# Local attention with a gated MoE layer: the attention's four PSUM banks as two tiles of two, its copies by tile, and the stages in a new order

## The chip, the cores and the metric

The kernel runs on one core of a Trainium2 chip. The metric is the device time of one execution in microseconds (us). The engines are TensorE (PE, matrix products), VectorE (DVE), ScalarE (ACT), GpSimd (POOL) and SyncE (SP, which issues the DMAs here). SBUF is the on-chip memory, PSUM the eight banks of 2 KB per partition into which TensorE writes.

## The reference, cut to what matters

For 8 batches of 8 heads, 512 local and 32 global positions and head size 64, attention with a window of 32 and global keys, then a gated layer on the joined heads:

```python
s_g  = scale * q_g @ k_all.T                    # 32 global queries see all 544 keys
out_g = softmax(s_g) @ v_all
s_ll = where(abs(i - j) <= 32, scale * q_l @ k_l.T, -1e9)
s_l  = concat([scale * q_l @ k_g.T, s_ll])      # local queries see a band and the 32 global keys
out_l = softmax(s_l) @ concat([v_g, v_l])
x = concat([out_g, out_l]) as [8, 544, 512]
h = relu(x @ w_in)                              # 512 -> 1024
conv = a depthwise filter of three taps along the sequence over h
out = (h * sigmoid(conv)) @ w_out               # 1024 -> 512
```

Here `x` is [8, 544, 512] because the 32 global rows and the 512 local rows of the 8 heads of 64 are joined.

## The kernel before, in words

The work is cut into small stages, each a function that issues some instructions; `n` counts heads (0 to 63, eight to a batch), `u` units of the gated layer, `o` its outputs. The attention of two heads at a time: LQ and LV load, **S** computes the scores (32 x 2 small matmuls into two banks, one for each head), **M** masks them on DVE out of PSUM (four operations with their row minimum, tile `negm`), **E** is the exp on ACT, **NS** and **NP** normalize (NP on POOL in the first batch, on ACT later), **DT** transposes blocks on DVE, **P** multiplies with the values (112 matmuls into four banks). The result of P is split into two fp32r parts: **XH** copies it on ACT into `xh`, **XL** subtracts on DVE into `xl`. For the global queries, once a batch: **G** (scores, four banks), **GM**, **GE**, **GN** (softmax), **GT** (transposes, two banks), **GC** (copy), **GP** (times values), **GO** (tile `og`), **GQ** (moves rows, into the bank beside GP's) and **GX** (splits them into `xh` and `xl`).

The gated layer: per batch and half of the sequence, eight units **PZ** (12 matmuls of 128 x 274 each, the product with `w_in` in three fp32r parts), **RE** (relu, ACT), **C1** (POOL), **Ca** and **Cb** (DVE; the three taps), **TH** (tanh, ACT, over two units), **GG** (DVE), **GH** (ACT) and **GL** (DVE or POOL; the split of `g`); then four outputs of two halves **Oa** and **Ob** (12 matmuls each), **OE** (copy, DVE) and **ST** (store). In the first 110 us, eight blocks of weights (`w_in`, then `w_out`) are loaded (WD) and split: WA, WH and WX on ACT, **WC** and **WL** on DVE, **WS** on PE.

All attention stages write one PSUM tile `four` of four banks (line 73), of which a planner hands out two halves of two banks. S, GT and GP take a half, G and P take both. The other four banks belong to a pool `ps` for PZ, O and WS. The tile framework derives the waits between instructions from the tiles they use.

The order of all stages on all engines is made ahead by a planner in the kernel (`plan`, `arranged`): each stage has an engine, a cost, predecessors, slots that it takes and frees, and a place from the tables `POS` (batches from the second on) and `POS0` (first batch and weights). `arranged` walks through time and starts on each engine the ready stage with the least place. `emit` issues the stages in that order and chains each engine's instructions in it; every engine, and SP's queue of DMAs, then runs strictly in order.

Of the kernel before, what the change touches and what calls it, by code (L numbers as in the profile page):

```python
# [11 lines left out]
F32 = mybir.dt.float32  # L12
# [6 lines left out]
P = 128  # L19
H = 8  # L20
# [31 lines left out]
def f(ap):  # L52
    return ap.bitcast(F32)
# [3 lines left out]
def attn_moe(ctx: ExitStack, tc: tile.TileContext, qk_d, vw_d, qg_d, w_in_d, w_out_d, cw_d, out_d):  # L57
# [221 lines left out]
    def SC(n):  # L279

        qk = heads[n]["qk"]
        k = SIDE["S", n] * 2
        for j in range(2):
            heads.setdefault(n + j, {})["s"] = four[:, k + j, :].rearrange("p (r x) -> p r x", r=NR)
        for r in range(NR):
            for c in range(4):
                i = NR * c + r
                a = SL + (NK * c + r) * SG
                for j in range(2):
                    rows = slice(j * D, (j + 1) * D)  # L290
                    nc.tensor.matmul(  # L291
                        heads[n + j]["s"][c * SG : (c + 1) * SG, r, :], lhsT=qk[rows, i * SG : (i + 1) * SG],
                        rhs=qk[rows, a : a + P], start=True, stop=True,
                    )

    def G(n):

        first = n - 7
        g = [groups.setdefault(2 * (n // H) + j, {}) for j in range(2)]
        for j in range(2):  # L300
            g[j]["s0"], g[j]["s1"] = four[:, j, :], four[:, 2 + j, 0:SG]
        for i in range(3):
# [68 lines left out]
    def XH(n):  # L371
        b, h = divmod(n, H)
        xh, xl = x_of(b, h // 2)
# [31 lines left out]

    def GT(n):
        gr = groups[n // 4]
        k = 2 * SIDE["GT", n]
        gr["t"] = four[:, k : k + 2, :].rearrange("p a x -> p (a x)")[:, 0 : NG * P]
# [9 lines left out]
    gos = {}  # L419

    def GP(n):
        b, k = n // H, 2 * SIDE["GP", n]
        po, pt = gos[b] = [four[:, k, 0 : 2 * D].rearrange("p (a d) -> p a d", a=2), four[:, k + 1, 0 : 4 * SG]]
# [123 lines left out]
    def ST(o):  # L547
# [2 lines left out]
        nc.sync.dma_start(out=out_d[b, mt, :, half * HALF : (half + 1) * HALF], in_=outs[o])  # L550

    emit(tc, B, dict(
        LQ=LQ, LV=LV, LG=LG, G=G, S=SC, M=MA, E=EX, NS=NS, NP=NP, DT=DT, P=PV, XH=XH, XL=XL,
        GM=GM, GE=GE, GN=GN, GT=GT, GC=GC, GP=GP, GO=GO, GQ=GQ, GX=GX,
        PZ=Z, RE=RE, C1=C1, Ca=lambda u: C2(u, 0), Cb=lambda u: C2(u, 2), TH=TH, GG=GG, GH=GH, GL=GL,
        Oa=lambda o: O(o, 0), Ob=lambda o: O(o, 1), OE=OE, ST=ST, WD=WD, WA=WA, WC=WC, WH=WH, WL=WL, WS=WS, WX=WX,
# [8 lines left out]
LIMIT = dict(h=2, o=2)  # L565

ENG = dict(
    XH="a", GC="a", GX="v", NP="a", RE="a", C1="p", GH="a", GL="v", OE="v", WA="a", WH="a", WX="a",
)
ENG0 = dict(  # L570
    XH="a", GC="a", GX="v", NP="p", RE="a", C1="p", GH="a", GL="p", OE="v", WA="a", WH="a", WX="a",
)

POS = dict(
    LQ=0.17, LG=-1.2, LV=8.05, S=-2.21, M=-18.29, E=219.57, NS=25.61, NP=295.34, DT=213.15, P=-133.05, XH=1.69,
    XL=-26.65, G=20.61, GM=45.55, GE=48.47, GN=-59.02, GP=-13.22, GX=48.92, PZ=21.78, RE=58.89, C1=-4.96,
    Ca=71.38, Cb=-23.21, TH=33.51, GG=-1.1, GH=-42.18, GL=39.36, Oa=143.85, Ob=115.21, OE=-11.46, ST=-82.81,
    WD=52.48, WA=25.01, WC=1.49, WH=74.51, WL=1.52, WS=45.66, WX=6.65, GC=38.39, GO=-50.79, GQ=16.06, GT=25.45,
)
# [14 lines left out]
def cost(key, e):  # L594
# [40 lines left out]
    if key == "NP":  # L635
# [29 lines left out]
def plan(B):  # L667
# [31 lines left out]
    for n in range(N):  # L699
# [26 lines left out]
        if h == H - 1:  # L726
            ks = [f"qk{p - 3 + c}" for c in range(4)]
            ga = ["ga%d" % b, "gb%d" % b]
# [22 lines left out]
def units(op, late, b):  # L751
    for half in range(2):
# [3 lines left out]
        for ft in range(NFT):  # L756
# [5 lines left out]
            ready = [("XL", 8 * b + h) for h in range(0, H, 2)]  # L762
# [13 lines left out]
        for mt in range(NCT):  # L776
# [7 lines left out]
            at_o("Ob", [("Oa", o), ("GL", 8 * hh + 5), ("GL", 8 * hh + 7)], [], [f"o{o}"] + g)  # L784
            at_o("OE", [("Ob", o)], [("o", f"ot{o}")], [f"o{o}", f"o{o}o"])
            at_o("ST", [("OE", o)], [], [f"ot{o}"])


def arranged(ops, sides=None):
# [26 lines left out]
    while events:  # L816
# [9 lines left out]
        for e in (PE, DVE, ACT, POOL, SP):  # L826
# [123 lines left out]
```

## Time and profile before

| | |
|---|---|
| median of 3 runs | 584.85 us (583.58, 584.85, 585.08) |
| the profiled execution | 582.82 us, its span 581.0 us |
| instructions | 23177 |
| PE busy | 548.5 us (94% of the span) |
| DVE busy | 428.9 us (74%) |
| ACT busy | 354.2 us (61%) |
| POOL busy | 99.3 us (17%) |

The span is the time from the first to the last instruction of the profiled execution. Busy time is a mean over stages with different limits; what waits for what is read stretch by stage. A row of waits says who waited, for whom, how long in total, how many times and the longest. In a timeline, a row gives the start, the duration, the engine, the line, the operation, and in brackets the idle time before it with what ended it.

### The profile page before, as it was taken

How to read it: one execution, taken by the hardware profiler on the slowest of the kernel's cores; microseconds unless marked ns; L12 is line 12 of the kernel's file. 1: busy time of each engine (PE TensorE's matmuls, PEld its weight loads, DVE VectorE, ACT ScalarE, POOL GpSimd, SP SyncE). 2: the span in 40 equal slices, each digit the busy share in tenths (PEclk: the TensorE clock that was granted, in tenths of full speed). 3: DMA queues.
4: the chain of work that ended last, by engine and by line, in shares of the span. 5: the costliest groups of instructions: out<-in, count | busy, mean ns of one | idle time of the engine just before them, and what ended most of it. 6: DMA issues, size and time to landing. Idle time of an engine off the chain costs nothing.

```text
span 581.0 us, 23177 instructions
## 1 busy us (share of the span) xinstructions
PE 548.5 (94%) x9904; PEld 511.8 (88%) x9904; DVE 428.9 (74%) x1371; ACT 354.2 (61%) x1108; POOL 99.3 (17%) x171
## 2 busy tenths in 40 slices
PE   3479999999999999999999899999999999999997
PEld 3356887889999899999999799999999899999997
DVE  3999999987785879757987588757878575646551
ACT  5657977858885597628973499419963583323420
POOL 3401241322011111201120012201111011111110
PEclk9989999999999999999999999999999999999999
DMA  8938432052322522116030613024000300000001
GB/s 351 371 135 325 154 129 99 17 156 104 113 79 71 169 90 84 62 37 225 12 124 23 209 52 113 28 61 151 23 18 25 108 21 20 22 21 30 20 30 48
DMA packets 20982, 57.07 MB, mean 98 GB/s; under 512 B 2448, under 2 KB 11664, under 8 KB 19856
## 3 DMA queue, kind: packets, MB, share of 16 engines
q1 hardware_dynamic: 20880, 55.61, 27.2%
q8 instruction: 77, 1.26, 0.9%
q14 instruction: 25, 0.20, 0.1%
HBM read 46.69 MB, written 8.91 MB: 96 GB/s over the span
## 4 chain that ended last, share of the span: by engine, by line
PE 81%; DVE 16%; issue 1%; DMA 1%; POOL 0%; ACT 0%; POOLq 0%; ACTq 0%
PE ps_o L538 33%; PE ps_h L475 30%; PE four L360 7%; PE four L291 5%; DVE pr L319 4%; PE four L412 2%; DVE t L499 2%; PE four L428 2%; DVE wt L125 1%; DVE pt L350 1%; PE four L312 1%; PE psw L223 1%; PE four L446 1%; DVE wt L122 1%; DMA qk<-qk 1%
## 5 line engine op out<-in xcount | busy, mean ns | idle before, releaser
L475 PE MATMUL ps_h<-xh,w_in 128*128 128x274 f32 x1024 | 221.9, 296 | 0.0
L538 PE MATMUL ps_o<-g,w_out 128*128 128x272 f32 x1536 | 212.7, 290 | 0.0
L538 PEld LDWEIGHTS ps_o<-g,w_out 128*128 128x128 f32 x1536 | 199.8, 188 | 0.8 <-issue 0.2
L475 PEld LDWEIGHTS ps_h<-xh,w_in 128*128 128x128 f32 x1024 | 169.3, 188 | 4.8 <-issue 3.0
L499 DVE SCALAR_TENSOR_TENSOR t<-hb,cw,t 128x272 f32<-128x272 f32 x256 | 126.0, 507 | 37.3 <-POOL t L275 35.9
L475 PE MATMUL ps_h<-xl,w_in 128*128 128x274 f32 x512 | 148.3, 290 | 0.0
L275 POOL TENSOR_SCALAR t<-hb,cw 128x272 f32<-128x272 f32 x128 | 75.3, 590 | 418.1 <-ACT hb L484 332.1
L329 ACT ACTIVATE pr<-pr,negm 128x128 f32<-128x128 f32 x256 | 99.3, 391 | 35.8 <-DVE negm L319 33.6
L475 PEld LDWEIGHTS ps_h<-xl,w_in 128*128 128x128 f32 x512 | 97.0, 189 | 0.0
L484 ACT ACTIVATE hb<-ps_h 128x273 f32<-128x273 f32 x128 | 50.5, 395 | 62.1 <-PE ps_h L475 60.7
L343 ACT ACTIVATE pr<-pr,sums 128x128 f32<-128x128 f32 x224 | 70.8, 394 | 0.3 <-DVE sums L337 0.3
L319 DVE CUSTOM_DVE_ANT_0 pr<-four,mask 128x128 f32<-128x128 f32 x256 | 57.2, 286 | 17.9 <-PE four L291 13.6
L508 ACT ACTIVATE t<-t 128x544 f32<-128x544 f32 x64 | 42.1, 657 | 37.8 <-DVE t L499 37.2
L360 PEld LDWEIGHTS four<-pt,vf 32*64 32x64 f32 x3584 | 48.8, 135 | 14.3 <-DVE negm L319 3.8
L360 PE MATMUL four<-pt,vf 32*64 32x96 f32 (+3 forms) x3584 | 52.6, 248 | 8.1 <-DVE negm L319 3.2
L240 ACT CAST g<-t 128x544 fp32r<-128x544 f32 x64 | 40.9, 643 | 24.9 <-DVE t L513 18.1
L291 PE MATMUL four<-qk 64*32 64x128 f32 x2048 | 40.9, 292 | 15.0 <-DVE negm L319 8.3
L513 DVE SCALAR_TENSOR_TENSOR t<-t,hb 128x544 f32<-128x544 f32 x64 | 45.9, 718 | 12.2 <-ACT t L508 12.2
L240 DVE COPY o<-ps_o 128x272 f32<-128x272 f32 x64 | 27.9, 437 | 31.3 <-PE ps_o L538 31.3
L350 DVE STREAM_TRANSPOSE pt<-pr 128x512 f32<-128x512 f32 x64 | 43.8, 697 | 9.6 <-PE four L360 7.3
L291 PEld LDWEIGHTS four<-qk 64*32 64x32 f32 x2048 | 31.1, 112 | 21.5 <-DVE negm L319 9.7
L329 ACT ACTIVATION_READ_ACCUMULATOR pr<-pr,negm 128x1 f32 x256 | 48.6, 190 | 0.0
(79 smaller groups left out, 398.8 us busy)
## 6 DMA issues: line engine op xcount, KB each, us to landing
qk<-qk SPq DMA_DIRECT2D x32, 704.0 KB, 5.4
vf<-vw SPq DMA_DIRECT2D x32, 448.0 KB, 5.8
out<-o SPq DMA_DIRECT2D x64, 136.0 KB, 1.8
raw<-w_in SPq DMA_DIRECT2D x4, 1024.0 KB, 13.2
raw<-w_out SPq DMA_DIRECT2D x4, 1024.0 KB, 5.7
qgf<-qg SPq DMA_DIRECT2D x8, 64.0 KB, 5.2
cwr<-cw SPq DMA_DIRECT2D x1, 24.0 KB, 13.4
```

Source lines behind the costliest of these rows:

```text
L240: nc.scalar.copy(out=out, in_=in_) if choice(key) == "a" else eng(key).tensor_copy(out=out, in_=in_)
L275: nc.gpsimd.tensor_scalar(out=out, in0=in_, scalar1=by, scalar2=0.0, op0=ALU.mult, op1=ALU.add)
L291: nc.tensor.matmul(heads[n + j]["s"][c * SG : (c + 1) * SG, r, :], lhsT=qk[rows, i * SG : (i + 1) * SG], rhs=qk[rows, a : a + P], start=Tr ...
L319: nc.vector.tensor_tensor_reduce(out=pr[:, r, :], in0=st["s"][:, r, :], in1=mask[:, r].rearrange("p a c -> p (a c)"), op0=ALU.add, op1=ALU ...
L329: nc.scalar.activation(out=st["p"][:, r, :], in_=st["p"][:, r, :], func=AF.Exp, scale=-1.0, bias=st["m"][:, r : r + 1], accum_out=two["r"] ...
L343: nc.scalar.activation(out=p[:, r, :], in_=p[:, r, :], func=AF.Copy, scale=by[:, r : r + 1])
L350: nc.vector.transpose(out=st["pt"].rearrange("p a q -> p (a q)"), in_=st["p"].rearrange("p r x -> p (r x)"))
L360: nc.tensor.matmul(four[j * D : (j + 1) * D, c, r0 * SG : (r1 + 1) * SG], lhsT=heads[n]["vf"][rows, j, m, :], rhs=heads[n + j]["pt"][rows, ...
L475: nc.tensor.matmul(ps, lhsT=w[:, ft, ct, :], rhs=x, start=i == 0, stop=i == 3 * NCT - 1)
L484: nc.scalar.activation(out=o, in_=z, func=AF.Relu, scale=0.5)
L499: nc.vector.scalar_tensor_tensor(out=st["t"], in0=st["h"][:, k : k + HALF], scalar=cw[:, 3 * ft + k : 3 * ft + k + 1], in1=st["t"], op0=AL ...
L538: nc.tensor.matmul(ps, lhsT=w[:, mt, ft, :], rhs=g[:, ft, :], start=ft + i == 0, stop=ft == NFT - 1 and i == 2)
```

## The change

The four banks become two tiles `four[0]` and `four[1]` of two banks. S, GT and GP write the tile that they are handed; G's large part goes to the first, its small one to the second; P writes all four banks as before, two in each tile. XH and XL, one operation each over four banks and 512 columns, become XH0, XH1, XL0 and XL1 over two banks and 256 columns, stages of their own, and each frees its own half. The planner hands out halves in a fixed order when both are taken. The tables `POS`, `POS0`, `LATE` and `WPOS` have new numbers.

```diff
-    four = ctx.enter_context(tc.tile_pool(name="four", bufs=1, space=PSUM)).tile([P, 4, 512], F32, name="four")
+    fours = ctx.enter_context(tc.tile_pool(name="four", bufs=1, space=PSUM))
+    four = [fours.tile([P, 2, 512], F32, name=f"four{k}") for k in range(2)]
...
-        k = SIDE["S", n] * 2
         for j in range(2):
-            heads.setdefault(n + j, {})["s"] = four[:, k + j, :].rearrange("p (r x) -> p r x", r=NR)
+            heads.setdefault(n + j, {})["s"] = four[SIDE["S", n]][:, j, :].rearrange("p (r x) -> p r x", r=NR)
...
-            g[j]["s0"], g[j]["s1"] = four[:, j, :], four[:, 2 + j, 0:SG]
+            g[j]["s0"], g[j]["s1"] = four[0][:, j, :], four[1][:, j, 0:SG]
...
-                        four[j * D : (j + 1) * D, c, r0 * SG : (r1 + 1) * SG], lhsT=heads[n]["vf"][rows, j, m, :],
+                        four[c // 2][j * D : (j + 1) * D, c % 2, r0 * SG : (r1 + 1) * SG], lhsT=heads[n]["vf"][rows, j, m, :],
...
-        cp("XH", xh[:, SG:S].rearrange("p (c x) -> p c x", c=4), four[:, :, 0:P])
-
-    def XL(n):
-        b, h = divmod(n, H)
-        xh, xl = [x[:, SG:S].rearrange("p (c x) -> p c x", c=4) for x in x_of(b, h // 2)]
-        nc.vector.tensor_tensor(out=xl, in0=four[:, :, 0:P], in1=f(xh), op=ALU.subtract)
+        return [x[:, SG + k * SL // 2 : SG + (k + 1) * SL // 2].rearrange("p (c x) -> p c x", c=2) for x in x_of(b, h // 2)]
+
+    def XH(n, k):
+        cp("XH%d" % k, two_of(n, k)[0], four[k][:, :, 0:P])
+
+    def XL(n, k):
+        xh, xl = two_of(n, k)
+        nc.vector.tensor_tensor(out=xl, in0=four[k][:, :, 0:P], in1=f(xh), op=ALU.subtract)
...
 POS = dict(
-    LQ=0.17, LG=-1.2, LV=8.05, S=-2.21, M=-18.29, E=219.57, NS=25.61, NP=295.34, DT=213.15, P=-133.05, XH=1.69,
+    LQ=21.27, LG=24.31, LV=2.19, S=13.51, M=35.08, E=92.2, NS=-31.19, NP=72.36, DT=60.36, P=-45.85, XH0=-20.03,
...
-            at_n("XH", [("P", e)], [], oo + [x], i=e)
-            at_n("XL", [("XH", e)], [], oo + [x], i=e)
+            for k in range(2):
+                at_n("XH%d" % k, [("P", e)], [], [oo[k], x], i=e)
+                at_n("XL%d" % k, [("XH%d" % k, e)], [], [oo[k], x], i=e)
...
+            if need_of(takes, "pa") == 2:
+                halves.sort()
```

What it does to the order is seen in three places. The first is the start of TensorE: the scores S of the first four pairs of heads, each with the semaphores that it waits for (DMAHW for its load, DVE for a masking). Before, the one tile is `four`:

```order
L291 MATMUL four<-qk 32x128 [waits DMAHW0_49]
L291 MATMUL four<-qk 32x128 x31
L291 MATMUL four<-qk 32x128 [waits DMAHW1_49,DVE_49]
L291 MATMUL four<-qk 32x128 x31
L291 MATMUL four<-qk 32x128 [waits DMAHW2_49,DVE_49]
```

After, the two tiles are `four_82` and `four_83`:

```order
L291 MATMUL four_82<-qk 32x128 [waits DMAHW0_49]
L291 MATMUL four_82<-qk 32x128 x31
L291 MATMUL four_83<-qk 32x128 [waits DMAHW1_49]
L291 MATMUL four_83<-qk 32x128 x31
L291 MATMUL four_82<-qk 32x128 [waits DMAHW2_49,DVE_49]
```

The second S waits for its load alone; the third, which writes the first tile again, still waits for DVE.

The second place is VectorE between the eighth masking and the fourth XL of the first batch; lines 121 to 125 are WC of a weight block (or, at 128x24, the same on the taps `cw`), 128 and 214 its WL, 350 is DT, 379 is XL. Before:

```order
L350 STREAM_TRANSPOSE pt<-pr 128x512
L379 TENSOR_TENSOR xl<-four,xh 128x512
L350 STREAM_TRANSPOSE pt<-pr 128x512
L121 TENSOR_SCALAR wt<-wt 128x1024
L122 TENSOR_SCALAR wt<-wt 128x1024
L125 SCALAR_TENSOR_TENSOR wt<-raw,wt 128x1024
L121 TENSOR_SCALAR cw<-cw 128x24
L122 TENSOR_SCALAR cw<-cw 128x24
L125 SCALAR_TENSOR_TENSOR cw<-cwr,cw 128x24
L128 TENSOR_SCALAR cwp<-cw 128x24
```

After (the lines of WC, WL and XL have moved down by one):

```order
L380 TENSOR_TENSOR xl<-four_82,xh 128x256
L350 STREAM_TRANSPOSE pt<-pr 128x512
L380 TENSOR_TENSOR xl<-four_83,xh 128x256
L350 STREAM_TRANSPOSE pt<-pr 128x512
L122 TENSOR_SCALAR wt<-wt 128x1024
L123 TENSOR_SCALAR wt<-wt 128x1024
L126 SCALAR_TENSOR_TENSOR wt<-raw,wt 128x1024
L350 STREAM_TRANSPOSE pt<-pr 128x512
L380 TENSOR_TENSOR xl<-four_82,xh 128x256
L380 TENSOR_TENSOR xl<-four_83,xh 128x256
```

The eight operations on `cw` are gone from here; they stand further ahead, between the second and the third DT. Each XL is two operations.

The third place is TensorE in the second batch, where GP (line 428), S (291) and GQ (446) meet. Before:

```order
L428 MATMUL four<-vf,pgt 32x64 x40
L291 MATMUL four<-qk 32x128 x32
L446 MATMUL four<-place,og 128x64 x2
L475 MATMUL ps_h<-xh,w_in_141 128x274
L475 MATMUL ps_h<-xl,w_in_141 128x274
```

After:

```order
L428 MATMUL four_83<-vf,pgt 32x64 x40
L291 MATMUL four_82<-qk 32x128 x32
L475 MATMUL ps_h<-xh,w_in_142 128x274
L475 MATMUL ps_h<-xl,w_in_142 128x274
...
L475 MATMUL ps_h<-xh,w_in_143 128x274
L446 MATMUL four_83<-place,og 128x64 x2
L475 MATMUL ps_h<-xh,w_in_142 128x274
L475 MATMUL ps_h<-xl,w_in_142 128x274
```

A whole PZ of 12 matmuls has come between S and GQ. In short, with Z for PZ, O for a half output, W for WS, T for GT, g for GP and q for GQ, TensorE's order up to the first O was `S S S S P W P P W P W G W S Z T Z W T Z S Z g Z W q Z Z G Z O` and is now `S S S S P W P P W P W S Z W Z G Z Z W Z T Z T Z G Z g S q W Z P Z O`.

## Rows read from the trace of the kernel before

**Rows 1.** The page's span, and the busy time, its share of the span and the number of instructions of each engine.

```profile
span 581.0 us, 23177 instructions
...
PE 548.5 (94%) x9904; PEld 511.8 (88%) x9904; DVE 428.9 (74%) x1371; ACT 354.2 (61%) x1108; POOL 99.3 (17%) x171
```

**Rows 2.** The busy time of each engine in stretches of the span (the stretch and its length, busy us and instructions of PE, of its weight loads, of DVE, ACT and POOL, the granted clock, DMA share, GB/s); the last row is from a cut into shorter stretches.

```profile
0.00:51.40 51.40, 30.77 (x848) 21.33 (x848) 40.24 (x135) 31.50 (x93) 12.28 (x35) 0.97 0.74 280
51.40:120.00 68.60, 66.48 (x1176) 58.19 (x1172) 64.71 (x191) 54.46 (x159) 21.16 (x23) 1.00 0.35 125
120.00:240.00 120.00, 117.58 (x2273) 111.11 (x2273) 93.72 (x353) 90.73 (x317) 20.14 (x31) 1.00 0.34 111
...
4.90:9.00 4.10, 2.15 (x72) 1.70 (x80) 1.78 (x16) 1.69 (x9) 0.00 (x0) 1.00 1.02 420
```

**Rows 3.** The waits of PE up to 51.4 us (who waited for whom, us in total, times, the longest).

```profile
PE four L291 <- DVE negm L319: 8.3, 3, 4.4
...
PE four L312 <- DVE xl L379: 1.1, 1, 1.1
```

**Rows 4.** The waits of PE from 51.4 to 120 us, all of them.

```profile
PE four L360 <- ACT pr L329: 1.6, 1, 1.6
PE four L412 <- DVE pg L404: 0.3, 1, 0.3
PE four L360 <- DVE pt L350: 0.2, 1, 0.2
```

**Rows 5.** The waits of PE from 120 to 560 us, all of them.

```profile
PE four L446 <- DVE og L437: 3.2, 6, 0.6
PE four L412 <- DVE negm L319: 1.6, 6, 0.6
PE four L291 <- issue: 0.9, 1, 0.9
PE four L291 <- DVE xl L456: 0.5, 1, 0.5
```

**Rows 6.** The timeline of PE at the start: the first two S, and the first matmul of the first PZ.

```profile
4.92 1.96 PE L291 MATMUL four<-qk 64*32 64x128 f32 x64 [4.92 <-DMA qk<-qk]
8.81 1.96 PE L291 MATMUL four<-qk 64*32 64x128 f32 x64 [1.93 <-DVE negm L319]
...
51.40 0.39 PE L475 MATMUL ps_h<-xh,w_in 128*128 128x274 f32 x1
```

**Rows 7.** The timeline of DVE at the start: the masking of the second pair of heads and its end, the first DT, and the first and the last operation on `cw`.

```profile
10.88 0.29 DVE L319 CUSTOM_DVE_ANT_0 pr<-four,mask 128x128 f32<-128x128 f32 x1 [2.12 <-PE four L291]
...
12.57 0.08 DVE L319 DVE_READ_ACCUMULATOR2_ANT negm<- 128x1 f32 x1
...
14.23 0.71 DVE L350 STREAM_TRANSPOSE pt<-pr 128x512 f32<-128x512 f32 x1 [1.26 <-POOL pr L345]
...
32.22 0.18 DVE L121 TENSOR_SCALAR cw<-cw 128x24 f32<-128x24 f32 x1
...
33.60 0.18 DVE L161 TENSOR_TENSOR cw<-cw,cwp 128x24 f32<-128x24 f32 x1
```

**Rows 8.** The timeline of PE in the second batch: GP, S and GQ.

```profile
120.31 1.32 PE L428 MATMUL four<-vf,pgt 128*32 128x64 f32 x80
121.57 1.16 PE L291 MATMUL four<-qk 64*32 64x128 f32 x64
123.26 0.66 PE L446 MATMUL four<-place,og 128*128 128x64 f32 x4 [0.54 <-DVE og L437]
```

**Rows 9.** The waits of all engines over the whole span, the row of GO.

```profile
DVE og L437 <- PE four L291: 7.3, 6, 2.0
```

**Rows 10.** Groups of instructions by line: engine, operation, out and in, shapes, count, then busy us and mean ns of one, then the idle time before them and what ended it.

```profile
L240 DVE COPY o<-ps_o 128x272 f32<-128x272 f32 x64 | 27.9, 437 | 31.3 <-PE ps_o L538 31.3
L379 DVE TENSOR_TENSOR xl<-four,xh 128x512 fp32r<-128x512 f32 x32 | 21.4, 670 | 13.1 <-ACT xh L240 13.0
...
L240 ACT CAST xh<-four 128x512 fp32r<-128x512 f32 x32 | 18.6, 583 | 35.0 <-PE four L360 34.9
```

**Rows 11.** The chain of work that ended last (start us, us, engine, tile, line, instructions): two half O after a P, a PZ after a P, a PZ among O's.

```profile
441.74 3.22 PE ps_o L538 x24
...
451.22 1.73 PE ps_h L475 x12
...
546.00 1.52 PE ps_h L475 x12
```

**Rows 12.** The end: the last twelve half O in the same chain, and the last GL in the timeline of DVE.

```profile
559.69 18.18 PE ps_o L538 x144
...
564.63 0.72 DVE L243 TENSOR_TENSOR g<-t,g 128x544 fp32r<-128x544 f32 x1
```

**Rows 13.** The timeline around the sixth WS: the last operation of its WL on DVE, and its first matmul on PE.

```profile
64.39 1.23 DVE L214 SCALAR_TENSOR_TENSOR w_out<-raw 128x1024 fp32r<-128x1024 uint32 x1
...
66.11 1.02 PE L223 MATMUL psw<-wt,ident 128*128 128x512 f32 x2
```

**Rows 14.** The page's DMA issues: the loads of qk (count, KB each, median us from issue to landing).

```profile
qk<-qk SPq DMA_DIRECT2D x32, 704.0 KB, 5.4
```

More of the change, by code (lines that the diff above doesn't have):

```diff
@@ L369, in x_of, with two_of @@
         return xs[b, ct]
-    def XH(n):
+    def two_of(n, k):
         b, h = divmod(n, H)
-        xh, xl = x_of(b, h // 2)
-        cp("XH", xh[:, SG:S].rearrange("p (c x) -> p c x", c=4), four[:, :, 0:P])
-    def XL(n):
-        b, h = divmod(n, H)
-        xh, xl = [x[:, SG:S].rearrange("p (c x) -> p c x", c=4) for x in x_of(b, h // 2)]
-        nc.vector.tensor_tensor(out=xl, in0=four[:, :, 0:P], in1=f(xh), op=ALU.subtract)
+        return [x[:, SG + k * SL // 2 : SG + (k + 1) * SL // 2].rearrange("p (c x) -> p c x", c=2) for x in x_of(b, h // 2)]
[4 more added lines that the diff above has]
+        nc.vector.tensor_tensor(out=xl, in0=four[k][:, :, 0:P], in1=f(xh), op=ALU.subtract)
     def GM(n):
@@ L407, in GT @@
         gr = groups[n // 4]
-        k = 2 * SIDE["GT", n]
-        gr["t"] = four[:, k : k + 2, :].rearrange("p a x -> p (a x)")[:, 0 : NG * P]
+        gr["t"] = four[SIDE["GT", n]].rearrange("p a x -> p (a x)")[:, 0 : NG * P]
         for s in range(NG):
@@ L421, in GP @@
     def GP(n):
-        b, k = n // H, 2 * SIDE["GP", n]
-        po, pt = gos[b] = [four[:, k, 0 : 2 * D].rearrange("p (a d) -> p a d", a=2), four[:, k + 1, 0 : 4 * SG]]
+        b, ps = n // H, four[SIDE["GP", n]]
+        po, pt = gos[b] = [ps[:, 0, 0 : 2 * D].rearrange("p (a d) -> p a d", a=2), ps[:, 1, 0 : 4 * SG]]
         for a in range(2):
@@ L552, in attn_moe @@
     emit(tc, B, dict(
-        LQ=LQ, LV=LV, LG=LG, G=G, S=SC, M=MA, E=EX, NS=NS, NP=NP, DT=DT, P=PV, XH=XH, XL=XL,
+        LQ=LQ, LV=LV, LG=LG, G=G, S=SC, M=MA, E=EX, NS=NS, NP=NP, DT=DT, P=PV,
+        XH0=lambda n: XH(n, 0), XH1=lambda n: XH(n, 1), XL0=lambda n: XL(n, 0), XL1=lambda n: XL(n, 1),
         GM=GM, GE=GE, GN=GN, GT=GT, GC=GC, GP=GP, GO=GO, GQ=GQ, GX=GX,
@@ L567 @@
 ENG = dict(
-    XH="a", GC="a", GX="v", NP="a", RE="a", C1="p", GH="a", GL="v", OE="v", WA="a", WH="a", WX="a",
+    XH0="a", XH1="a", GC="a", GX="v", NP="a", RE="a", C1="p", GH="a", GL="v", OE="v", WA="a", WH="a", WX="a",
 )
 ENG0 = dict(
-    XH="a", GC="a", GX="v", NP="p", RE="a", C1="p", GH="a", GL="p", OE="v", WA="a", WH="a", WX="a",
+    XH0="a", XH1="a", GC="a", GX="v", NP="p", RE="a", C1="p", GH="a", GL="p", OE="v", WA="a", WH="a", WX="a",
 )
 POS = dict(
-    LQ=0.17, LG=-1.2, LV=8.05, S=-2.21, M=-18.29, E=219.57, NS=25.61, NP=295.34, DT=213.15, P=-133.05, XH=1.69,
@@ L576 @@
-    XL=-26.65, G=20.61, GM=45.55, GE=48.47, GN=-59.02, GP=-13.22, GX=48.92, PZ=21.78, RE=58.89, C1=-4.96,
-    Ca=71.38, Cb=-23.21, TH=33.51, GG=-1.1, GH=-42.18, GL=39.36, Oa=143.85, Ob=115.21, OE=-11.46, ST=-82.81,
-    WD=52.48, WA=25.01, WC=1.49, WH=74.51, WL=1.52, WS=45.66, WX=6.65, GC=38.39, GO=-50.79, GQ=16.06, GT=25.45,
+    LQ=21.27, LG=24.31, LV=2.19, S=13.51, M=35.08, E=92.2, NS=-31.19, NP=72.36, DT=60.36, P=-45.85, XH0=-20.03,
+    XH1=-24.04, XL0=-84.19, XL1=27.81, G=-99.41, GM=-28.05, GE=-48.6, GN=-28.85, GP=-16.21, GX=70.71, PZ=23.1,
@@ L579 @@
+    RE=-45.29, C1=-34.59, Ca=-15.91, Cb=45.79, TH=55.28, GG=114.13, GH=-10.39, GL=46.36, Oa=35.47, Ob=199.2,
+    OE=-49.23, ST=52.01, WD=-31.51, WA=183.61, WC=-70.22, WH=29.26, WL=-3.99, WS=-26.62, WX=30.76, GC=20.39,
+    GO=3.38, GQ=29.11, GT=85.66,
 )
 POS0 = dict(
-    LQ=-54.32, LG=122.32, LV=24.61, S=11.66, M=-269.6, E=18.63, NS=-371.65, NP=31.19, DT=27.79, P=-92.39,
-    XH=-64.38, XL=90.88, G=73.46, GM=5.67, GE=-5.13, GN=27.22, GP=-9.32, GX=-68.82, PZ=162.76, RE=0.4, C1=39.48,
-    Ca=19.32, Cb=-15.01, TH=-18.64, GG=13.41, GH=-4.29, GL=-67.07, Oa=700.61, Ob=26.93, OE=5.01, ST=75.51,
@@ L584 @@
-    WD=178.21, WA=20.85, WC=349.86, WH=11.43, WL=20.5, WS=24.18, WX=358.1, GC=19.28, GO=30.1, GQ=53.87, GT=62.82,
-)
-LATE = (127.37, -0.94)
-WPOS = [-113.51, -211.25, -194.88, -55.49, 70.06, -0.06, 31.31, 203.22]
+    LQ=-173.08, LG=68.82, LV=-68.25, S=-16.95, M=44.99, E=22.61, NS=-9.13, NP=-74.18, DT=40.66, P=-8.59,
+    XH0=14.96, XH1=3.56, XL0=-14.52, XL1=47.8, G=24.73, GM=-47.2, GE=-8.24, GN=32.97, GP=-12.83, GX=-73.69,
+    PZ=-11.97, RE=-56.44, C1=38.76, Ca=-21.63, Cb=-23.36, TH=-51.23, GG=-29.29, GH=-95.57, GL=7.81, Oa=-8.13,
@@ L589 @@
+    Ob=-34.65, OE=-18.97, ST=-29.21, WD=-53.99, WA=-101.3, WC=427.44, WH=-0.47, WL=236.4, WS=11.82, WX=34.96,
+    GC=-22.28, GO=-54.86, GQ=-12.23, GT=52.86,
+)
+LATE = (38.5, 42.93)
+WPOS = [-70.72, -65.89, -7.27, 17.44, 18.44, 19.1, 97.6, 44.26]
 LAST_BATCH = 7
@@ L639, in cost @@
         S=pe(890), P=pe(1400), G=pe(980), GT=pe(560, 250), GP=pe(1430), GQ=pe(250), PZ=pe(1522), Oa=pe(1508), Ob=pe(1508),
-        M=(830, 910), E=(1544, 1550), NS=(400, 480), DT=(606, 690), XL=two(SL), GM=(930, 1010), GE=(733, 750),
+        M=(830, 910), E=(1544, 1550), NS=(400, 480), DT=(606, 690), XL0=two(SL // 2), XL1=two(SL // 2), GM=(930, 1010), GE=(733, 750),
         GN=(740, 820), GO=(360, 440), GX=(4 * 350, 4 * 350 + 80), RE=(290, 395) if e == "a" else psum(273),
@@ L644, in cost @@
     )[key]
-COPIES = dict(XH=(SL, 1), GC=(5 * P, 1), GH=(2 * HALF, 0), OE=(HALF, 1), WH=(1024, 0), WX=(1024, 1))
+COPIES = dict(XH0=(SL // 2, 1), XH1=(SL // 2, 1), GC=(5 * P, 1), GH=(2 * HALF, 0), OE=(HALF, 1), WH=(1024, 0), WX=(1024, 1))
 DIFFERENCES = dict(GL=2 * HALF)
@@ L741, in plan @@
             at_n("GQ", [("GO", n)], [], [gp, og])
-            at_n("GX", [("GQ", n)] + [("XL", n - 7 + 2 * c) for c in range(4)], [], [gp] + [f"x{b},{c}" for c in range(4)])
+            at_n("GX", [("GQ", n)] + [("XL%d" % k, n - 7 + 2 * c) for c in range(4) for k in range(2)], [], [gp] + [f"x{b},{c}" for c in range(4)])
             units(op, late, b)
@@ L760, in at_u @@
                 op(key, u, late(H + u // 2 + u % 2 * 0.5, b) + (POS if b else POS0)[key], b > 0, *more)
-            ready = [("XL", 8 * b + h) for h in range(0, H, 2)]
+            ready = [("XL%d" % k, 8 * b + h) for h in range(0, H, 2) for k in range(2)]
             ready += [("GX", 8 * b + 7)] * (half == 0) + [weight(ft // 2)]
@@ L786, in units, with need_of @@
             at_o("ST", [("OE", o)], [], [f"ot{o}"])
+def need_of(takes, kind):
+    return sum(k == kind for k, _ in takes)
 def arranged(ops, sides=None):
```

## The prediction

> **What bounds the kernel now.** I read the share of busy time first: TensorE is busy for 548.5 us of a span of 581.0, VectorE for 428.9 [rows 1]. So I ask where TensorE's 32 us of idle time lie, and what sets its pace there. The stretches [rows 2] split them: 20.6 us before 51.4 us, 2.1 from there to 120, 6.2 from 120 to 560 (the sum of [rows 5]), and about 3.1 at the end, when the last output leaves. The reader should see three regimes. Up to 51.4 us, where the first full matmul group of the MoE part starts [rows 6], TensorE waits for VectorE. From 51.4 to 120 both are nearly full: VectorE 64.7 and TensorE 66.5 of 68.6 us. After that VectorE has slack (93.7 of 120) and TensorE is the bound: only its own work, and small waits, count.
>
> The waits of each regime carry names. At the start it is the scores S that wait for the masking M (negm), 8.3 us in three waits [rows 3]. In the second regime it is one P (1.6 us) and little more [rows 4]. In the third it is the small matmul q, which waits for og six times (3.2 us in all), the transpose T, which waits for negm six times (1.6), and single waits of S [rows 5].
>
> **The change, part by part.** I call the matmul stages by the names in the code: S, P, G, g (that is GP), q (GQ), T (GT), Z (PZ), O, W (WS).
>
> *No matmul is removed or added*: 128 Z, 128 half O, 32 S, 32 P, 8 W and so on stand in both orders. The gain can only be idle time, and the loss only idle time or a stage that runs longer in another neighbourhood.
>
> *Start.* Before, the second S starts at 8.81 us, in the very moment when VectorE ends the first masking [rows 6], although it writes the other half; the masking of its heads then starts at 10.88, after 2.12 us in which VectorE is idle [rows 7]. In the new order that wait on DVE is gone and only the DMA is left. 704 KB at the 420 GB/s of this stretch [rows 2] are 1.7 us behind the first landing at 4.9, so about 6.6; the S can follow the first at once, from 6.9 to 8.9. Masking then ends at about 10.7, not 12.65. What follows is a chain through ACT (exp), VectorE, POOL (normalize) and VectorE (transposes), where VectorE waits once more (the transpose at 14.23 was 1.26 us late). The new order puts the eight tiny operations on cw, which stood from 32.22 to 33.7 [rows 7], into that stretch; they hide part of a wait and are 1.5 us less later. I walk it: the eighth masking ends some 0.4 us earlier than before, and after the cw operations' old place VectorE is 0.4 + 1.5 = 1.9 us ahead.
>
> *Copies by halves.* XL of 512 columns takes 670 ns, a copy of 272 columns out of PSUM takes 437 [rows 10]; so two halves take at most 0.87 against 0.67, and by their share of columns not less than 0.67. I take +0.1 to +0.15 a pair. Over 32 pairs that is 3 to 5 us of VectorE; after 120 us its 26 us of idle time in 120 hide it. Ahead of the first Z lie four pairs: 0.4 us on the path. Twice 256 on ACT instead of 583 ns [rows 10] falls into ACT's idle time.
> [...]
>
> Start in all: 1.9 - 0.4 = **1.5 us gained**. The bounds: nothing, if the second qk lands after 8.8; 2.6, if the wait for POOL shrinks as well. In exchange the new order runs S and a Z before the fourth W and before G. This only swaps work that TensorE has anyway.
>
> *Second regime.* Here the order is new: by the sixth W TensorE has done eight Z, not five, and a second G, a q and no fewer T: about 6.0 us more. VectorE has, ahead of the WL which that W needs, two more groups of GM (0.92 each), four more C (0.44), two more DT (0.64), one GG (0.65), and small ones: about 6.5 us. Before, that WL ended at 65.6 and the W began at 66.11 [rows 13], with TensorE just behind VectorE. Shift both: VectorE 65.6 + 6.5 - 1.5 = 70.6, and TensorE would be there at 66.1 + 6.0 - 1.5 = 70.6. The small q ahead of it waits for GO, which stands behind that WL on VectorE: 0.35 more. I expect waits of about 0.3 to 1.0 there, and 0.4 at the G that must wait for both copies of T: 1.5 us in place of 2.1, so **0.6 gained**, with bounds from 2 us gained (nothing waits) to 4 us lost (each us of VectorE's delay is paid in full here).
> On SP the fifth qk now stands behind the first w_out load, which waits for the first weight block's slot until about 26.5; with 5.4 us to landing [rows 14] it is there by 32 or 33, and S needs it at 45. That costs nothing. The later loads stand in front of the same users as before.
>
> *Third regime.* Six times the old order has g, S, q. In the trace g runs from 120.31, S from 121.57, and q waits 0.54 us [rows 8]. The reason is on VectorE: og, which q needs, itself waited 7.3 us in six times for the S between them [rows 9], though S writes the other half. The new order has g, S, Z, q: with two tiles og needs only g, and a Z of 1.5 us lies ahead of q. All 3.2 us go. T's six waits for masking (1.6) go as well where T's half isn't the one being masked; where it is, two Z now lie between. The waits of S, 0.5 on xl and 0.9 on "issue", I halve. New risks are P, O, P (once), and T, Z, P (twice), where the copies of a half or of T have 1.5 to 1.7 us and need about 1.2 to 2.2. I set 1.7 us of waits in place of 6.2: **4.5 gained**; bounds 6.2 (none left) and 0 (as many new).
>
> *Neighbours.* Every stage or group of small stages between full ones costs extra: two half O after P take 3.22 us, where twelve in a row take 18.18 [rows 12], 3.03 for two; a Z after P takes 1.73, one among O's 1.52 [rows 11]. So about 0.2 for each interruption. I count 85 interruptions in the old order and 90 in the new one (q stands alone now): 5 x 0.2 = **1.0 lost**.
> [...] The rows here show P alone beside full stages and cannot tell T and q apart from it; I keep the loss.
>
> *End.* After the last Z six half O's used to cover the chain to the last GL; it ended at 564.63 + 0.72 = 565.35, 5.8 us after that Z [rows 12]. Now four cover it, 6.06 us. That still hides it; 0 to 0.3 lost, I take nothing.
>
> **Sum.** -1.5 - 0.6 - 4.5 + 1.0 = -5.6 us. The profiled execution took 582.82 us with a span of 581.0, so 577.2. The runs' median is 584.85, 2.0 above it (their spread is 1.5 us); the difference carried to it gives **579.3 us**. A measurement of this kernel tells about 0.3% from no change, that is 1.75 us.
>
> **The rivals.**
> *The waits move (same).* A new order has as many small waits in the third regime as the old one, because P, O, P and T, Z, P leave less room. For it: three such places are tighter by a us or more. Against it: the two largest groups, og and negm, come from the shared tile. Time: only the start and the second regime count, 1.5 + 0.6 - 1.0 = 1.1 gained, 583.7.
> *VectorE falls behind at the sixth W (slower).* The place: the WL behind eight Z's worth of C, GG and the second GM. Its forecast end of 70.6 is the very time at which TensorE gets there. Each us later is a us of the kernel, since VectorE's 95% leave no room to catch up before 120. From 5.6 us late on (76.2) the gain is gone, from 7.4 it is slower by over 0.3%; a chain of exp, normalize and Relu on ACT in this stretch that holds VectorE up for 8 us would give 587. For it: ACT does 3 us of exp between the first two Relus. Against: ACT was busy only 54 of these 68.6 us.
> *More is freed (faster still).* VectorE's maskings also waited for TensorE on the shared tile, so it runs ahead more than I walk: the second regime loses its 2.1, the third its 6.2, the start 2.0: 9.3 in all after the 1.0 lost, 575.5.
> *The two tiles do nothing.* If the waits of S and og on the other half were real (the data, not the tile), they'd stay. But the new order's second S has no wait for DVE at all, so this is near nothing.
>
> **How the numbers follow.** Forecast (2 to 7 us gained) 0.60; more freed 0.13; waits move 0.15; VectorE behind 0.12. Faster by over 0.3% (below 583.1): 0.60 + 0.13 = 0.73; within: 0.15; slower: 0.12. The range leaves out the slower case and half of the one that frees more: 576.5 to 585.0, where the upper end takes in the third regime's bound of no gain and half of the second's loss.
>
> **What would show each step.** Start: the second S at about 7 us, not 8.8; the first Z at about 46 us. Second regime: TensorE idle under 2.5 us to 120; the sixth W at 70 to 72. Third: no q waits for og, and T's waits for negm under 0.5 us in all; the sum of TensorE's waits from 120 to 560 below 2.5 us. Neighbours: TensorE's busy time up by about 1 us. End: no idle TensorE between the last Z and the last O. The prediction is wrong if TensorE shows waits of 3 us or more between 51 and 120, or if the third regime shows new waits for xl or pgt of the size of those removed.

## The result, and the profile after

The changed kernel takes 574.66 us (median of 4, 573.74 to 575.49) where the kernel before took 584.35 on the same chip (583.58 to 585.08): ratio 0.9834, 95% interval 0.9812 to 0.9856. That is 9.7 us faster. The forecast was 5.6 faster, 579.3, with 576.5 as its lower end: the direction came out as written, and so did the waits that went, but not the size, and the time lies below the range. The profiled execution took 573.74 us.

The page and the stretches after, in the form of [rows 1, 2]:

```profile
span 572.0 us, 23262 instructions
...
PE 546.3 (96%) x9904; PEld 511.7 (89%) x9904; DVE 431.0 (75%) x1403; ACT 355.1 (62%) x1140; POOL 97.3 (17%) x171
```

```profile
0.00:51.40 51.40, 31.16 (x820) 22.24 (x821) 42.10 (x146) 33.09 (x109) 12.74 (x36) 0.83 0.75 283
51.40:120.00 68.60, 67.30 (x1287) 58.65 (x1287) 62.85 (x191) 53.78 (x157) 19.63 (x22) 1.00 0.36 124
120.00:240.00 120.00, 119.33 (x2236) 113.19 (x2218) 97.31 (x361) 92.08 (x323) 18.00 (x32) 1.00 0.32 110
```

TensorE is idle for 0.7 us of the 120 after 120 us, where it was 2.4. All waits of PE from 51.4 to 120, and after them all from 120 to 560 (compare [rows 4, 5]):

```profile
PE four L360 <- DVE negm L319: 0.6, 1, 0.6
PE four L291 <- DVE xl L380: 0.4, 1, 0.4
PE four L446 <- DVE gsum L403: 0.2, 1, 0.2
```

```profile
PE four L291 <- issue: 0.4, 1, 0.4
PE ps_h L475 <- issue: 0.3, 1, 0.3
PE four L446 <- issue: 0.2, 1, 0.2
```

The twelve waits of q and T are gone, and the three that are left in the third regime name no engine. At the start, in the form of [rows 6]: the first three S, the first matmul of the first Z, and the q ahead of the sixth W with that W.

```profile
4.84 3.50 PE L291 MATMUL four<-qk 64*32 64x128 f32 x128 [4.84 <-DMA qk<-qk]
8.74 1.16 PE L291 MATMUL four<-qk 64*32 64x128 f32 x64 [0.40 <-DVE negm L319]
...
46.13 0.39 PE L475 MATMUL ps_h<-xh,w_in 128*128 128x274 f32 x1
...
70.30 0.63 PE L446 MATMUL four<-place,og 128*128 128x64 f32 x4 [0.24 <-DVE gsum L403]
70.76 1.08 PE L224 MATMUL psw<-wt,ident 128*128 128x512 f32 x2
```

The second S no longer waits: its 64 matmuls stand in one row with the first's. Up to 51.4 us this left TensorE hardly less idle (20.2 us, before 20.6), because the wait went on to P, which also writes the banks that the maskings read: P waited 3.2 us for negm before, and now

```profile
PE four L360 <- DVE negm L319: 10.5, 2, 6.6
```

The eighth W is the last stage that both orders reach with nearly the same work behind them. It starts at 107.35, before at 109.59: 2.24 us gained. From there to the end of the last matmul of O it took 461.43 us, before 468.26: 6.83 gained. Behind that O lie 3.2 us in both. 2.24 + 6.83 = 9.07 us, the difference between the spans (581.0 and 572.0, each rounded). The forecast had 2.1 for the first piece and 4.5 - 1.0 = 3.5 for the second, so the miss lies in the third regime. The eighth W and the row of the last O, before and then after:

```profile
109.59 1.02 PE L223 MATMUL psw<-wt,ident 128*128 128x512 f32 x2
...
559.53 18.32 PE L538 MATMUL ps_o<-g,w_out 128*128 128x272 f32 x144
```

```profile
107.35 1.02 PE L224 MATMUL psw<-wt,ident 128*128 128x512 f32 x2
...
553.48 15.30 PE L538 MATMUL ps_o<-g,w_out 128*128 128x272 f32 x120
```

### The profile page after: what moved, and what is told of

It reads as the page before. It is cut to its first block, busy times and chain, and to the rows that moved or that the text cites. A ratio compares the mean times of both kernels' runs of the same rounds, so it can differ in the third digit from the quotient of the medians.

```text
span 572.0 us, 23262 instructions
## 1 busy us (share of the span) xinstructions
PE 546.3 (96%) x9904; PEld 511.7 (89%) x9904; DVE 431.0 (75%) x1403; ACT 355.1 (62%) x1140; POOL 97.3 (17%) x171
## 4 chain that ended last, share of the span: by engine, by line
PE 87%; DVE 8%; DMA 2%; issue 1%; ACT 1%; SPq 0%; DVEq 0%; ACTq 0%
PE ps_o L538 34%; PE ps_h L475 34%; PE four L360 7%; PE four L291 5%; DMA raw<-w_in 2%; PE four L428 2%; PE four L312 2%; PE four L412 1%; PE psw L224 1%; DVE pr L319 1%; DVE t L499 1%; DVE pt L350 1%; DVE xl L380 1%; DVE wt L126 1%; PE four L446 1%
## 5 line engine op out<-in xcount | busy, mean ns | idle before, releaser
L276 POOL TENSOR_SCALAR t<-hb,cw 128x272 f32<-128x272 f32 x128 | 74.0, 584 | 395.4 <-ACT hb L484 247.8
L291 PE MATMUL four<-qk 64*32 64x128 f32 x2048 | 39.1, 282 | 8.9 <-DMA qk<-qk 4.8
L244 DVE TENSOR_TENSOR g<-t,g 128x544 fp32r<-128x544 f32 x56 | 40.3, 722 | 6.0 <-ACT g L241 5.5
```

The lines of the kernel that those rows point to most:

```text
L276: nc.gpsimd.tensor_scalar(out=out, in0=in_, scalar1=by, scalar2=0.0, op0=ALU.mult, op1=ALU.add)
L291: nc.tensor.matmul(heads[n + j]["s"][c * SG : (c + 1) * SG, r, :], lhsT=qk[rows, i * SG : (i + 1) * SG], rhs=qk[rows, a : a + P], start=Tr ...
```

## The experiments

Three kernels took the change apart, one turned a step of its order back, three moved single stages of the old order on two tiles, one put a wait back, and three are repeats. Each ratio is against runs of the kernel before in the same set.

**The tiles alone.** The kernel before, its order tables and stages untouched, with `four` as two tiles. XH and XL become two operations each, inside the same stage.

```diff
-    four = ctx.enter_context(tc.tile_pool(name="four", bufs=1, space=PSUM)).tile([P, 4, 512], F32, name="four")
+    fours = ctx.enter_context(tc.tile_pool(name="four", bufs=1, space=PSUM))
+    four = [fours.tile([P, 2, 512], F32, name=f"four{k}") for k in range(2)]
```

> The old order of stages, unchanged, on two tiles of two banks (XH and XL as two operations each, in the same stage and place). Theory A, the shared tile is the cause: at the start the second S goes at 7 us and VectorE is 2 us earlier, 0.4 of it eaten by the halves; from 120 us on og no longer waits for S, so q's 3.2 us and T's 1.6 us of waits go, and with them what a wait costs beyond its idle row (weight loads that can't go ahead: 4.8 against 3.2 us for q, 2.9 against 1.6 for T in the rows of the weight loads). Sum 1.6 + 7.7 = 9.3 at most, 7 as the middle: 577 us. Theory B, the new order is the cause: only the start gains, 1.6 us: 582.7 us, with q still waiting about 0.3 each time.

Measured: 571.95 us, ratio 0.9801 (0.9784 to 0.9818), span 570.8. All waits of PE from the eighth W on:

```profile
PE four L291 <- issue: 0.7, 2, 0.3
```

The tiles alone remove every wait for og and negm there, in the old order, and do more than the whole change. The gain of 11.6 us is more than the 9.3 that theory A gave at most. By the profiles, which are 10.2 apart, 7.63 of it lie behind the eighth W, where 7.7 was the bound, and 2.57 ahead of it (3.16 and 3.38 in the repeats), where 1.6 was expected. Two repeats gave 572.24 and 572.19 us; their expectations stand further down.

**The order alone.** The changed kernel with one tile of four banks again, of which `four[0]` and `four[1]` are views.

```diff
-    fours = ctx.enter_context(tc.tile_pool(name="four", bufs=1, space=PSUM))
-    four = [fours.tile([P, 2, 512], F32, name=f"four{k}") for k in range(2)]
+    whole = ctx.enter_context(tc.tile_pool(name="four", bufs=1, space=PSUM)).tile([P, 4, 512], F32, name="four")
+    four = [whole[:, 2 * k : 2 * k + 2, :] for k in range(2)]
```

> The new order of stages with its split copies, on one tile of four banks again. Theory A: the waits on the other half come back. The second S goes at 8.8 us (2 us later); each S behind g, and each T, waits for VectorE's work on the other half, some of it now covered by the Z between: 3 to 8 us more than the changed kernel, 578 to 583 us. Theory B: 576 to 577 us, only the start's 2 us are lost.

Measured: 589.62 us, ratio 1.0108 (1.0088 to 1.0127): slower than the kernel before, and 6.6 us beyond the upper end of theory A. Against the kernel before, 1.1 us are lost ahead of the eighth W (110.68) and 5.7 behind it (473.94 to the last O). Three of its waits of PE from 120 to 560 us:

```profile
PE four L446 <- DVE negm L319: 3.6, 5, 1.1
PE four L412 <- DVE negm L319: 2.6, 4, 1.0
PE four L412 <- ACT pgt L241: 1.1, 3, 0.5
```

A Z ahead of q did not help it here, where the masking of the S beside it counts as a use of q's tile: q waited 3.6 us in five times for the masking, longer than the 3.2 in six that it waited for og in [rows 5].

**The copies alone.** One tile, old order, XH and XL cut into two halves each.

```diff
-        cp("XH", xh[:, SG:S].rearrange("p (c x) -> p c x", c=4), four[:, :, 0:P])
+        for k in range(2):
+            cp("XH", two_of(n, k)[0], four[:, 2 * k : 2 * k + 2, 0:P])
```

> The old order on one tile; only XH and XL are split into two operations of half the columns. Both theories: VectorE has 0.09 us more for each pair of heads, 0.3 to 0.4 us of it ahead of the first Z, and hides the rest: 584.4 to 585.2 us. If fixed costs per instruction were on the path all through (32 pairs at 0.1 to 0.15), 587 to 589 us.

Measured: 584.76 us, ratio 1.0021 (1.0005 to 1.0036); the span is 1.0 longer, the first Z starts at 51.78 and not 51.40. The 0.4 us of the forecast is what the four pairs ahead of it cost. In the changed kernel a half takes 411 ns in the mean, against 670 for the whole [rows 10]:

```profile
L380 DVE TENSOR_TENSOR xl<-four,xh 128x256 fp32r<-128x256 f32 x64 | 24.2, 411 | 5.9 <-ACT xh L241 5.5
```

**q behind S again.** The changed kernel, where S Z q becomes S q Z.

```diff
+        if (ops[x][0], ops[y][0], ops[z][0]) == ("S", "PZ", "GQ"):
+            row.remove(y)
+            row.insert(row.index(z) + 1, y)
```

> The changed kernel with one thing moved: in seven batches the Z between S and q is issued behind q, so that g, S, q stand together as they did before. Theory that an interruption of full stages costs 0.2 us whatever stage it is: six or seven interruptions fewer, 1.2 to 1.4 us faster than the changed kernel (573.3 us), if og is ready in time; with two tiles og waits for g alone, 0.4 us after g against 1.1 us of S, so q waits for nothing. [...] If og is late all the same, q waits 0.3 to 0.5 us each time: 576 to 577 us.

It came to six places, not seven. Measured: 574.33 us, ratio 0.9842 (0.9826 to 0.9858), no difference from the change. In both kernels the pieces from g to the stage behind the second Z are 6.03 to 6.04 us long in two places of the six, and up to 6.8 and 7.0 in the others, with gaps that name no engine; the sums of six are 38.1 in the change and 38.5 here. In the undisturbed ones q between Z takes 0.36 instead of 0.47, and the two Z, which it parts, take that 0.1 more. So no cost of q standing alone shows.

**The two orders on two tiles, side by side.** The first kernel of this list and the changed kernel, unedited, on one chip.

> The old order on two tiles once more, beside the changed kernel on the same chip, since the two were 571.95 and 574.66 us in different sets of runs, each against its own runs of the kernel before. Theory 'the new order costs' (the stages stand in more and shorter groups, and each group beside full matmul stages costs about 0.2 us): 572.0, the changed kernel 1 to 3 us above it, with a span some 1.2 us longer. Rival 'no difference': both within 0.8 us of each other.

> The changed kernel itself beside the old order on two tiles. By 'the new order costs' 573 to 575 us and 1 to 3 us above that one. By 'no difference' within 0.8 us of it.

Measured: 572.24 us (0.9806, 0.9784 to 0.9828) and 575.33 us (0.9846, 0.9821 to 0.9871). The intervals of this pair overlap a little, but three sets of the one (0.9801, 0.9806, 0.9802) and two of the other (0.9834, 0.9846) lie apart: the new order costs 2 to 3 us on two tiles. By the profiles some of it lies ahead of the eighth W (107.35 and 108.35 against 107.02, 106.43 and 106.21) and some behind it (461.43 and 462.55 us to the last O against 460.63, 460.82 and 460.73). The 1.0 us between the first two starts came with a granted clock of 0.69 in the one profile and 0.50 in the other from 26 to 30 us, as the last section shows, so the profiles don't fix how much of the 2 to 3 us belongs to the order itself.

**A gap more.** The tiles alone, with g S q Z turned into g Z S q; it came to six places, not seven.

```diff
+        if (ops[x][0], ops[y][0], ops[z][0], ops[w][0]) == ("GP", "S", "GQ", "PZ"):
+            row.remove(w)
+            row.insert(row.index(y), w)
```

> The price of an interruption by itself: the old order on two tiles, where in seven batches the Z behind g S q is moved in between g and S (g Z S q in place of g S q Z). No work is added, and no wait is expected: og has a Z and an S to be ready in. Theory 'each side of a full stage that touches a small one costs 0.1 us': that Z rises from 1.63 to 1.73 us and the stage behind q gets the 0.1 that Z had there, 0.2 a place, seven places, so +1.2 to 1.4 us against the old order on two tiles (573.2). Rival 'groups of small stages cost the same split or whole', which is what the changed kernel with q moved showed for q: no difference, 572.0. Should S being 1.5 us later make its masking late, a wait for negm shows at the next S or T.

Measured: 572.35 us, ratio 0.9801 (0.9785 to 0.9818): no difference. Yet the place itself grew. PE of the tiles alone, and after it of this kernel, from g to the next S:

```profile
117.72 1.32 PE L430 MATMUL four<-vf,pgt 128*32 128x64 f32 x80
118.98 1.16 PE L291 MATMUL four<-qk 64*32 64x128 f32 x64
120.06 0.66 PE L448 MATMUL four<-place,og 128*128 128x64 f32 x4
120.53 0.37 PE L477 MATMUL ps_h<-xh,w_in 128*128 128x274 f32 x1
...
123.75 1.16 PE L291 MATMUL four<-qk 64*32 64x128 f32 x64
```

```profile
117.79 1.32 PE L430 MATMUL four<-vf,pgt 128*32 128x64 f32 x80
119.04 0.39 PE L477 MATMUL ps_h<-xh,w_in 128*128 128x274 f32 x1
...
120.77 1.16 PE L291 MATMUL four<-qk 64*32 64x128 f32 x64
121.85 0.66 PE L448 MATMUL four<-place,og 128*128 128x64 f32 x4
...
124.00 1.16 PE L291 MATMUL four<-qk 64*32 64x128 f32 x64
```

6.03 us became 6.21, the 0.2 expected, and from the eighth W on the Z and O are 1.1 to 1.3 us longer in sum than in the three profiles of the base. But irregular gaps inside S, which gave its 24 stages there 1.3 to 1.5 us more than 24 times 1.09 in the base, are absent here. They come and go between kernels, and what causes them stays open. So the price of an interruption by S shows in the rows, and these gaps hide it in the time.

**A gap less.** The tiles alone, S Z T turned into S T Z, in seven places (not nine); then in the last six of them alone, with a third repeat of the base.

```diff
+        if (ops[x][0], ops[y][0], ops[z][0]) == ("S", "PZ", "GT"):
+            row.remove(y)
+            row.insert(row.index(z) + 1, y)
```

> The other way round: the old order on two tiles, where S Z T becomes S T Z in nine places, so that T stands with S and one Z less has a small stage ahead of it. By '0.1 us a side' 9 times 0.11 us are saved, 1.0 us, 571.0. By 'split or whole, the same' 572.0. If T, now 1.5 us earlier, comes before its softmax (pg) or the masking of its half is done, new waits of T show and the time is 572 to 574.

> The old order on two tiles a third time, as the base of the two beside it: 572.0, span 570.4 to 570.8.

> The old order on two tiles with S Z T made S T Z in the six batches after the weights, not at the first T, which in the run before waited 2.1 us for its softmax and so gave back what the rest saved. If that one wait was the whole loss, the stretch from the last W to the last O stays at 459.5 us, as in the run before, against 460.6 to 460.8, and the time is 1.1 us below the base beside it (570.9). If the 1.1 us was chance, no difference.

Measured: 572.12 us (0.9806, 0.9787 to 0.9825) in seven places; base 572.19 (0.9802, 0.9788 to 0.9817), last six places 571.78 (0.9797, 0.9783 to 0.9812). With all seven the first T waited:

```profile
52.20 1.33 PE L414 MATMUL four<-ident,pg 128*128 128x128 f32 x5 [2.08 <-DVE pg L407]
```

Without that place the stretch from the last W to the last O is 459.85 us against 460.73, close to what was expected, but the time moved only 0.4 us, which these intervals don't tell from none.

**A wait put back.** The tiles alone, g S q turned into g q S in six batches.

```diff
+        if (ops[x][0], ops[y][0], ops[z][0]) == ("GP", "S", "GQ"):
+            row.remove(y)
+            row.insert(row.index(z) + 1, y)
```

> The cost of a wait against its own row: the old order on two tiles with q right behind g in six batches (g q S in place of g S q), so that q waits for og (0.42 us long) with nothing between. Expected row: q waits for og six times, 0.5 to 0.6 each, 3.3 in all. Theory 'a wait costs its idle row': the stretch from the last W to the last O becomes 3.3 us longer than the base's 460.7, so 464.0, time 575.3. Theory 'a wait costs about a fifth to a third more than its row' (the stage behind it starts slower): 464.7 to 465.1, and 576.0 to 576.4; the pieces g to Z then are longer by more than the idle time in them.

Measured: 576.16 us, ratio 0.9871 (0.9854 to 0.9887), 4.0 above the base beside it. Its waits for og, on the matmuls and on the weight loads:

```profile
PE four L448 <- DVE og L439: 4.0, 6, 0.8
```

```profile
PEld four L448 <- DVE og L439: 4.9, 6, 0.9
```

The wait's row came out longer than the 3.3 expected, and the time grew by as much as the row, 4.0 for 4.0; the stretch from the last W grew by 3.5. But that isn't the price of the wait alone. The six pieces from g to the Z behind S grew from 2.81 (undisturbed) to between 3.54 and 3.75, with 0.55 to 0.75 idle: 0.19 a place more than the idle time in five of the six, 0.07 in g and 0.12 in q, and 0.36 in the other. That is the sign that the theory of a surcharge named. At the same time the irregular gaps inside S, 1.6 us in the base beside it, are absent here as in the kernel with a gap more. So the two theories aren't told apart, nor is it shown whether the 0.19 belongs to the wait or to q standing right behind g.

## Why the prediction missed

**Start: right in its mechanism, too large in its size.** The second S followed the first, and the first Z started at 46.13 (about 46 was written). But the 1.5 us were to be VectorE's lead, and that can be read at the fourth XL, ahead of which VectorE does the same work in both orders, but for the halves. Before and after:

```profile
45.65 0.68 DVE L379 TENSOR_TENSOR xl<-four,xh 128x512 fp32r<-128x512 f32 x1
```

```profile
44.58 0.42 DVE L380 TENSOR_TENSOR xl<-four,xh 128x256 fp32r<-128x256 f32 x1
```

The lead is 1.07 us, and 0.05 in the repeat of the changed kernel (45.60), where the first Z started at 47.16. The walk to 1.9 was wrong on the way: the eighth masking ended at 24.99, 0.8 later than before and not 0.4 earlier, and the operations on cw, which were to hide part of a wait, waited 0.7 for ACT themselves.

**Second regime: right in its signs, too small in its size.** TensorE was idle for 1.3 of the 68.6 us above (1.5 was taken); the sixth W started at 70.76 (70 to 72 was written), and the q ahead of it waited 0.24 of the 0.3 to 1.0 allowed. The slower rival, VectorE late at this W, did not come. From the fourth XL to the eighth W 1.2 us were gained, in the repeat too, where 0.6 was forecast. That the two terms together gave 2.2 in the profile for the 2.1 forecast was luck: one was too large and the other too small, and in the repeat the sum is 1.2.

**Third regime: the term that failed.** The 4.5 us were taken as 6.2 us of idle time less 1.7 that would remain. What remained was 0.9. And the waits had cost more than their idle rows: the term measured 7.6. This can be read without the new order, between the kernel before and the tiles alone: the same stages in the same order took 468.26 and 460.63 us, 7.6 us less, for idle rows of 6.2 and 0.7. PE before, from S to the Z behind the first T of the second batch, and after it the same with the tiles alone:

```profile
127.08 1.16 PE L291 MATMUL four<-qk 64*32 64x128 f32 x64
...
130.19 0.77 PE L412 MATMUL four<-ident,pg 128*128 128x128 f32 x5 [0.22 <-DVE negm L319]
130.71 0.38 PE L475 MATMUL ps_h<-xh,w_in 128*128 128x274 f32 x1
```

```profile
123.75 1.16 PE L291 MATMUL four<-qk 64*32 64x128 f32 x64
...
126.46 0.71 PE L414 MATMUL four<-ident,pg 128*128 128x128 f32 x5
126.93 0.37 PE L477 MATMUL ps_h<-xh,w_in 128*128 128x274 f32 x1
```

3.63 us became 3.18: 0.45 gained where the row shows 0.22 idle. The piece g S q, of [rows 8], was 3.42 us to the next Z and is 2.81: 0.61 for a row of 0.54. That Z, before:

```profile
123.73 0.37 PE L475 MATMUL ps_h<-xh,w_in 128*128 128x274 f32 x1
```

The rest of such a wait hides in the busy time of the stages beside it. The view that could have shown it is that of the weight loads, whose row for this q is 0.80 us long where the matmuls' is 0.54. Those of before, from 120 to 560 us:

```profile
PEld four L446 <- DVE og L437: 4.8, 6, 0.8
...
PEld four L412 <- DVE negm L319: 2.9, 6, 0.8
...
PEld four L291 <- DVE xl L456: 2.2, 6, 0.7
```

9.9 us, where the matmuls' own rows for the same three have 5.3 [rows 5]. What the tiles gave back lies between the two sums. In the places that no irregular gap disturbs, the truth was near the matmuls' row for og and near the loads' for T, so no fixed factor is shown.

**Neighbours: wrong in its count.** The 1.0 us was five interruptions at 0.2, counted because q stands alone now. But q alone among Z cost nothing that shows: the ratio is 0.9834 with it there and 0.9842 with it behind S again. For S set between full stages the 0.2 a place holds in the rows (6.03 us became 6.21 in the kernel with a gap more). The sign that was named, TensorE's busy time up by about 1 us, did not come: it fell from 548.5 to 546.3. By the profiles the new order does cost something on two tiles, 0.6 to 1.9 us in this stretch, but part of that is irregular gaps, so the term is neither shown nor refuted in size, and which edit of the order costs the 2 to 3 us stays open.

**Copies and end: right.** A pair of halves took 0.82 us in the mean against 0.67, 0.4 us on the path to the first Z, and no time beyond the last Z was lost.

The rival "more is freed" (575.5) was nearest, but not by its route: the start and the second regime together gave no more than was forecast, the third alone more. That the order was taken as a source of the gain is the other error: removing the shared tile gave it, and the new order took some back. The upper end of the range doesn't follow from its own words: 579.3 and 4.5 are 583.8, and half of a loss of 4 us makes 585.8, not 585.0; nothing here hangs on it.

## What to carry to other kernels

Here two engines that used different halves of one tile waited for each other through it: GO waited 7.3 us in six times for an S in the other half [rows 9]. Look in the trace for a wait whose releaser works on another part of the same buffer, and split the tile before rearranging stages. Size such a gain with two views, the matmuls' idle rows and the weight loads' waits; here the gain (7.6 us) lay between their sums (5.3 and 9.9). When a change has two parts, time each alone: here one (with the copies by halves) was worth 11.5 us and the other less than nothing.

## What the runs showed of the hardware

The same S took different times with nothing in the rows to say why: before, the 64 matmuls of each of the first two S took 1.96 us [rows 6], later ones 1.16 [rows 8]; after, the third S took 1.16 already at 8.74 us, 0.40 behind the first two. The granted clock reads 1.00 from 4.9 to 9 us in both kernels, and from 120 to 240 us before.

With two tiles the four S are done earlier, TensorE pauses for longer behind them (6.6 us at the longest, where it was 4.4), and the granted clock there fell to 0.50, where it had stayed at 1.00. The stretches from 18 to 30 us, before and then after:

```profile
18.00:22.00 4.00, 1.96 (x64) 1.51 (x64) 3.93 (x15) 3.94 (x17) 0.00 (x0) 1.00 1.05 420
22.00:26.00 4.00, 1.74 (x90) 1.74 (x97) 3.93 (x21) 3.72 (x16) 2.42 (x2) 1.00 1.01 394
26.00:30.00 4.00, 4.00 (x50) 2.29 (x36) 3.96 (x7) 1.59 (x5) 2.11 (x3) 1.00 0.82 272
```

```profile
18.00:22.00 4.00, 0.70 (x8) 0.30 (x8) 3.93 (x21) 3.54 (x14) 0.00 (x0) 0.50 1.01 411
22.00:26.00 4.00, 0.95 (x45) 0.96 (x53) 3.93 (x21) 3.63 (x16) 1.64 (x2) 0.50 0.50 202
26.00:30.00 4.00, 4.00 (x79) 2.76 (x73) 3.96 (x7) 2.36 (x10) 2.43 (x3) 0.69 0.28 55
```

TensorE did 1.65 us of work from 18 to 26 us, where it had done 3.70. In this profile no loss can be read from it: VectorE, for which TensorE waits here, is full in these rows (11.8 of 12 us in both).

In other profiles of the same stages it does cost time. In the repeat of the changed kernel the clock still read 0.50 from 26 to 30 us, under the first W and the P behind it:

```profile
26.00:30.00 4.00, 4.00 (x77) 2.71 (x68) 3.96 (x8) 1.80 (x8) 2.43 (x3) 0.50 0.31 51
```

There the first W took 5.04 us (27.22 to 32.26), where it had taken 3.43 (27.27 to 30.70), and VectorE had to wait for that P, which it had not:

```profile
DVE pt L350 <- PE four L360: 1.0, 1, 1.0
```

This 1.0 us is still there at the first Z (47.16 for 46.13) and at the eighth W (108.35 for 107.35). The tiles alone show the same a stage later: the clock was 0.50 from 34 to 38 us and 0.76 from 38 to 42 (0.66 and 0.92 before), the second W took 4.84 us (3.58 before), VectorE waited 0.9 us for ACT behind it, and the first Z started at 50.80, only 0.60 earlier than before; in the kernel with the wait put back, which has the same order up to there, the clock read 0.60 and then 1.00, the second W took 3.57, VectorE had no such wait, and the first Z started at 49.70.
